# When the whole blocks of the second weights are stored: by rounding progress, or in four fixed steps

## The chip, the cores and the metric

The kernel runs on one core of a Trainium2 chip. The metric is the device time of one launch in microseconds, as the median of several runs; lower is better.

## The reference

Inputs are q, k, v of shape 8 x 8 x 576 x 64 (batch, heads, rows, width), and two weight matrices in float64, 512 x 2048 and 2048 x 512. Three things are computed, one after the other:

```
attention in chunks of 64 rows:  out = softmax(q k^T / 8) v        per head and chunk
x = out, heads side by side                                        8 x 576 x 512
u = x + Re(FFT over rows and columns of x)
y = u + relu(layernorm(u) @ w_ch1) @ w_ch2
```

All results are float32, while the weights arrive as float64.

## The kernel before, in words

**Tiles and groups.** The 8 x 576 rows are cut into tiles of 128 rows. Tiles are joined into nine groups of four, `g` = 0 to 8; groups 0 to 7 hold the main tiles of one batch each, the last holds the left-over rows of all batches. For each group the two matmuls of the MLP ("up" with the first weights, "down" with the second) run on PE, and between their parts the attention and the Fourier stage of the *next* batch are woven in by hand.

**Steps.** `mlp(g)` is a generator that yields after each part of a group's matmuls. The main loop counts these yields in `t` and, in the body of each step, lets the other work of that step be issued. For group 0 the steps 1 to 16 are parts of "up" (L1219) and the steps 17 to 32 are the 16 blocks `m` of "down" (L1260), so that block `m` comes just before the body of step 17 + `m`. `begin[1]` is 32, `ready_at[0]` is 27. Nothing is reordered afterwards: each engine and each DMA queue gets its instructions in the order in which the bodies issue them, and waits are set by the data and the spaces they touch.

**Rounding the weights.** The float64 weights are loaded in 32 pieces of 128 x 512 (512 KB each, L348, issued by SP): pieces 0 to 15 are the first weights, piece 16 + `m` is block `m` of the second weights. `round_weight(i)` turns a piece into float32 with instructions on DVE (L372, L379, L380, L382, L388) and ACT (L364, L367, L370); its first half treats piece `i`, its second half finishes piece `i - 1`, whose raw space then takes the next load. The last pieces have only three raw spaces, in the rows of `xall`. `n_w` is the number of the next call of `round_weight`. In most steps there are one or two such calls; in step 23 one of them stands inside the Fourier stage of batch 1, ahead of `z_joined` (L752).

**The products with fewer multiplications.** From group 1 on (for "up") and group 2 on (for "down") the kernel multiplies in 2 x 2 blocks with seven products instead of eight, and later with fewer still. It needs the blocks of the second weights in DRAM (`s2`): three of the seven are plain blocks of the weights, four are sums of them.
- `keep2_whole(i)` (L1109) stores the three plain blocks for the rows `m` = 2`i`, 2`i` + 1 and 8 + 2`i`, 9 + 2`i`, with three DMAs of 256 KB from SP (L1114). Called W0 to W3 below. The rows must have been rounded.
- `keep2(i)` makes the four sums on POOL (L1095) in spare rows: of `xall`, which are the raw spaces of the last weight pieces, or of `yall`. `keep2_store` (L1107) stores them from SP in a later step. `keep2(1)` begins in the first step whose `n_w` is over 32.
- `keep1(p)` (L1078, POOL) makes sums of the first weights, writing them into the place of the second weights' blocks 0 to 11 (`keep1(0)`: blocks 0 to 2); `keep1_store` (L1082, SP) stores one block of the first weights. Such a store in step 24, say, is called K24.

**Where the whole blocks are stored.** The stores of `keep2_whole(i)` are issued in the step in which `n_w` passes 26 + 2`i`, after that step's roundings and before its `keep2_store` and `keep1_store`. More than one `i` may fall into a step.

**The rest around it.** In steps 23 to 27 the Fourier stage of batch 1 ends: its halves are joined on DVE (L752, L756), copied by ACT (L747, L773 to L778), multiplied on PE (`mix`, L840), copied and joined by ACT (L845) and DVE (L850, L851), added to x by DVE or POOL (L857), and normalized (L705 to L710, L998). The normalized rows are transposed on PE (L399) for group 1.

Of the kernel before, what the change touches and what calls it, by code (L numbers as in the profile page):

```python
# [16 lines left out]
def kernel(  # L17
# [43 lines left out]
    KF = DFF // 128  # L61
# [41 lines left out]
    NO, HF = 7, KF // 2  # L103
# [918 lines left out]
    def combined(g, q_, late=False):  # L1022

        unT = unTs[g]
        cl, ch = slice(q_ * 128, (q_ + 1) * 128), slice(256 + q_ * 128, 256 + (q_ + 1) * 128)
        b11, b12, b21, b22 = unT[:, 0:2, cl], unT[:, 0:2, ch], unT[:, 2:4, cl], unT[:, 2:4, ch]
        t1, t2, t4 = (tt_1[o][:, :, cl] if g == 1 else tt[:, o, :, cl] for o in range(3))
        if late:
            nc.vector.tensor_tensor(out=t4, in0=b21, in1=t2, op=ALU.subtract)
            return  # L1030
        nc.vector.tensor_tensor(out=t1, in0=b12, in1=b11, op=ALU.subtract)
        nc.vector.tensor_tensor(out=t2, in0=b22, in1=t1, op=ALU.subtract)
        nc.vector.tensor_tensor(out=b12, in0=b22, in1=b12, op=ALU.subtract)
        if g > 1:
            nc.vector.tensor_tensor(out=t4, in0=b21, in1=t2, op=ALU.subtract)
# [35 lines left out]
    def keep1(pair):  # L1071

        a11, o2, o1, a21, a12, o4, a22 = parts1(pair)
        for out_, in0, in1, op in (
            (o1, a21, a22, ALU.add), (o2, o1, a11, ALU.subtract),
            (a21, a11, a21, ALU.subtract), (o4, a12, o2, ALU.subtract),
        ):
            nc.gpsimd.tensor_tensor(out=out_, in0=in0, in1=in1, op=op)  # L1078

    def keep1_store(pair, o):  # L1080
        to = s1[pair, o].rearrange("p (k x) -> p k x", k=2)
        nc.sync.dma_start(out=to, in_=parts1(pair)[o])  # L1082
# [19 lines left out]
    def keep2_store():  # L1102
        to = s2.rearrange("o p (m e) -> o p m e", m=HF)
        while kept:
            m, made = kept.pop(0)
            for o, a in made:
                nc.sync.dma_start(out=to[o, :, m:m + 2], in_=a)  # L1107

    def keep2_whole(i):  # L1109

        m = 2 * i
        to = s2.rearrange("o p (m e) -> o p m e", m=HF)
        for o, m0, e0 in ((0, m, 0), (4, HF + m, 0), (5, HF + m, HM)):
            nc.sync.dma_start(out=to[o, :, m:m + 2], in_=w2[:, m0:m0 + 2, e0:e0 + HM])  # L1114
# [60 lines left out]
    def fetch(which):  # L1175
        i = n_slab[which]
        if which == 1 and i < HF // 2 * NO * (NG - 2):
            pair, o = divmod(i % (HF // 2 * NO), NO)
            nc.sync.dma_start(out=slab1[i % NS1].rearrange("p k r f -> p (k r f)"), in_=s1[pair, UP[o]])
        elif which == 3 and i < NR2 * (NG - FEW):  # L1180
            to = slab3[i % NS3].rearrange("p m e -> p (m e)")
            nc.sync.dma_start(out=to, in_=block_of(PRODUCTS[i % NR2][1]))
        elif which == 2 and i < NO * (FEW - first_of[2]):
            nc.sync.dma_start(out=slab2[i % NS2].rearrange("p m e -> p (m e)"), in_=s2[i % NO])
        n_slab[which] = i + 1
# [267 lines left out]
    def mlp(g):  # L1453

        for h1 in up_halves(g) if g >= first_of[1] else up_plain(g) if g > 0 else up_first():
            yield
        yield from (down_few if g >= FEW else down_halves if g >= first_of[2] else down_plain)(g, h1)

    with tc.manual_schedule():
# [22 lines left out]
        n_w = 2  # L1482
# [10 lines left out]
        def round_next(later=None):  # L1493
            nonlocal n_w
            if n_w <= len(pieces):
                round_weight(n_w, later)
                n_w += 1
# [25 lines left out]
        ready_at = [begin[g] + (2 * KF - 5 if g < first_of[2] else 2 * HF + 4) for g in range(NG)]  # L1523
# [12 lines left out]
        n_whole, n_kept, late, rest_ = 0, 0, [], None  # L1536
        conv2 = chain(conv2)
        t = 0
        for g in range(NG):
            for _ in mlp(g):  # L1540
                t += 1
                heavy = False
                for do in late:
                    do()
                late = []
                if t == 8:
                    nc.scalar.copy(tk, early_tk[:, :, :, 0:NE])
                if cur < len(sides):
                    t0 = 3 if cur == 0 else ready_at[cur - 1]
                    t1 = ready_at[cur]  # L1550
                    due = min(sizes[cur], (t - t0) * sizes[cur] // (t1 - t0))
                    if cur == 0:
                        due = late_due.get(t, (t - t0) * sizes[cur] // (t1 - 2 - t0))
                    while done < due:
                        heavy = next(sides[cur], None) or heavy
                        done += 1
                    if t >= t1:
                        for _ in sides[cur]:
                            pass
                        cur, done = cur + 1, 0  # L1560
                while joined:
                    combined(*joined.pop(0))
                if not heavy:
                    round_next(late if t < KF and t % 4 == 3 else None)
                    if t <= 2 or t < KF and t % 4 == 0 or t >= KF + 3:
                        round_next()

                while n_whole < HF // 2 and n_w > KF + HF + 2 * n_whole + 2:
                    keep2_whole(n_whole)
                    n_whole += 1  # L1570
                keep2_store()
                if n_w > len(pieces):
                    for _ in range(3):
                        next(conv2, None)
                if t == begin[1] - 1:
                    for _ in conv2:
                        pass
                    keep2_store()
                if begin[1] < t < begin[1] + 7 and t % 2:
                    keep1((t - begin[1] + 1) // 2)  # L1580
                if t == ready_at[FEW - 1]:
                    rest_ = make_rest()
                if t >= ready_at[FEW - 1]:
                    next(rest_, None)
                if t == begin[FEW] + 2 * HF - 2:
                    for _ in rest_:
                        pass
                    slab3.extend(
                        one_p.tile([128, Z3], FP32, tag=tag, name="more").rearrange("p (m e) -> p m e", m=4)
                        for tag in ("q", "k")  # L1590
                    )
                for _ in range((2, 3, 10, 11, 12, 12, 13, 13, 14, 15).count(t - begin[FEW])):
                    fetch(3)
                for _ in range(2 if t > begin[1] else 0):
                    if put_off:
                        b, t0_, r, o = put_off.pop(0)
                        nc.sync.dma_start(out=out[b, t0_ + 1 - r:t0_ + CH:2, :], in_=o)
                if KF < t <= KF + 4 or KF + 8 <= t < KF + 16:
                    keep1_store(n_kept // 3, (0, 4, 6)[n_kept % 3])
                    n_kept += 1  # L1600
                if begin[1] <= t < begin[1] + KF:
                    keep1_store((t - begin[1]) // 4, (2, 1, 3, 5)[(t - begin[1]) % 4])
                if t in (begin[1] + 9, begin[1] + 13, begin[1] + 16):
                    fetch(2)
                if t == begin[1] + KF:
                    for _ in range(NS1):
                        fetch(1)
# [49 lines left out]
```

## Time and profile before

| | |
|---|---|
| median of 3 runs | 1063.99 us (1063.61 to 1064.34) |
| the profiled execution | 1063.73 us, span on the core 1061.9 us |
| PE busy | 1043.3 us, 98% of the span |
| DVE busy | 626.5 us, 59% |
| POOL busy | 431.9 us, 41% |
| ACT busy | 315.5 us, 30% |
| bytes moved by DMA | 219.10 MB, mean 206 GB/s |
| stores of whole blocks (L1114) | 12, issued from 140.4 to 160.9 us of the span |

The span is the time in which the core's engines work; the run's time holds 1.8 us more around it. Times of the views are counted from the span's start. A matmul in float32 stands in the profile as more than one instruction: one block of "down", four matmuls, has eight.

### The profile page before, as it was taken

What the parts mean: (1) busy time and instruction counts of PE and PEld (TensorE: products, weight loads), DVE (VectorE), ACT (ScalarE), POOL (GpSimd) and SP (SyncE); (2) the same over time, 40 slices, a digit from 0 to 9 for tenths busy, and PEclk for the clock granted to TensorE, in tenths of its full rate; (3) what the DMA queues carried; (4) which work ended last, traced back from release to release, by engine and by line L of the source; (5) the groups of instructions that cost most, each with busy time, mean ns of one, the idle gap of its engine ahead of it and who ended that gap; (6) DMA issues with size and microseconds to landing.
All of it is one profiled execution on the core that took longest, in us unless ns stands there. A gap on an engine that the chain in (4) does not pass through costs nothing.

```text
span 1061.9 us, 20222 instructions
## 1 busy us (share of the span) xinstructions
PE 1043.3 (98%) x7482; PEld 851.6 (80%) x7482; DVE 626.5 (59%) x1339; ACT 315.5 (30%) x744; POOL 431.9 (41%) x555
## 2 busy tenths in 40 slices
PE   7999999999999999999999999999999999999998
PEld 6645444788888888888888888888888888888887
DVE  4798986974567465664565645745664666443332
ACT  4688573233113311332022312331133103201200
POOL 3410119753425151244134421514252777660282
PEclk9999999999999999999999999999999999999999
DMA  8767675687688447973678357944753759998364
GB/s 169 221 197 213 163 218 199 203 233 230 231 215 230 134 142 214 250 207 108 186 229 223 118 169 231 250 131 155 215 168 102 269 187 353 363 399 279 89 216 142
DMA packets 167088, 219.10 MB, mean 206 GB/s; under 512 B 77228, under 2 KB 111020, under 8 KB 161614
## 3 DMA queue, kind: packets, MB, share of 16 engines
q1 hardware_dynamic: 155978, 211.98, 64.8%
q0 software_dynamic: 9024, 4.91, 2.1%
q8 instruction: 60, 0.98, 0.4%
q10 hardware_dynamic: 1988, 0.92, 0.3%
q14 instruction: 38, 0.31, 0.1%
HBM read 183.61 MB, written 34.08 MB: 205 GB/s over the span
## 4 chain that ended last, share of the span: by engine, by line
PE 79%; DVE 6%; DMA 4%; ACT 3%; POOL 3%; SPq 2%; issue 2%; DVEq 0%; ACTq 0%; POOLq 0%
PE pa L1309 20%; PE pb L1309 15%; PE pb L1363 14%; PE pa L1363 11%; PE dn L1427 7%; PE pt L399 2%; SPq L265 2%; PE mix L840 2%; PE xp L501 2%; PE z L722 1%; DMA xall<-in_moe_w_ch_dram 1%; PE up L1219 1%; PE sc L451 1%; POOL h L1207 1%; POOL part L1156 1%
## 5 line engine op out<-in xcount | busy, mean ns | idle before, releaser
L1309 PE MATMUL pa<-unT,wa 128*128 128x256 f32 x736 | 175.3, 381 | 0.2 <-DVE xall L1317 0.2
L1309 PEld LDWEIGHTS pa<-unT,wa 128*128 128x128 f32 x736 | 138.1, 190 | 19.6 <-DVE xall L1317 0.6
L1309 PE MATMUL pb<-wa 128*128 128x256 f32 x448 | 106.6, 381 | 0.0
L1309 PEld LDWEIGHTS pb<-wa 128*128 128x128 f32 x448 | 84.3, 190 | 11.5
L1363 PE MATMUL pa<-wb,h 128*128 128x256 f32 x384 | 87.2, 380 | 0.0
L1363 PE MATMUL pb<-wb,h 128*128 128x256 f32 x384 | 86.4, 379 | 0.0
L1193 POOL TENSOR_TENSOR h<-h 128x256 f32<-128x256 f32 x48 | 40.8, 858 | 98.2 <-DVE wb L1191 91.6
L1363 PEld LDWEIGHTS pa<-wb,h 128*128 128x128 f32 x384 | 71.8, 190 | 9.7
L1363 PEld LDWEIGHTS pb<-wb,h 128*128 128x128 f32 x384 | 72.0, 190 | 9.4
L1044 POOL DMA_DIRECT2D out_dram<-wb x28 | 18.8, 674 | 121.8 <-DVE wb L1380 71.9
L1315 DVE TENSOR_TENSOR wa<-pb,wa 128x256 f32<-128x256 f32 x56 | 23.7, 424 | 63.5 <-ACT wa L1314 63.5
L1309 PE MATMUL pb<-unT,wa 128*128 128x256 f32 x256 | 60.6, 379 | 0.1
L1325 ACT ACTIVATE h<-pa 128x256 f32<-128x256 f32 x64 | 24.6, 384 | 115.0 <-PE pa L1309 114.1
L1260 PE MATMUL dn<-wb,h 128*128 128x512 f32 x128 | 58.7, 608 | 0.0
L1314 ACT COPY wa<-pa 128x256 f32<-128x256 f32 x56 | 20.9, 372 | 121.4 <-PE pa L1309 121.4
L1309 PEld LDWEIGHTS pb<-unT,wa 128*128 128x128 f32 x256 | 48.6, 190 | 7.1 <-DVE wa L1315 0.5
L1207 POOL TENSOR_TENSOR h<-h 128x512 f32<-128x512 f32 x34 | 42.8, 1276 | 27.2 <-ACT h L1331 24.1
L1309 PE MATMUL pa<-wa 128*128 128x256 f32 x224 | 53.9, 383 | 0.0
L483 ACT COPY pT<-pt 128x512 f32<-128x512 f32 x36 | 21.0, 582 | 105.8 <-PE pt L399 105.5
L1331 ACT ACTIVATE h<-h 128x512 f32<-128x512 f32 x64 | 40.0, 630 | 39.5 <-DVE h L1330 39.1
L1219 PE MATMUL up<-unT,wa 128*128 128x512 f32 x108 | 49.4, 598 | 0.0
L857 POOL TENSOR_TENSOR xall<-y,xall 128x513 f32<-128x513 f32 x14 | 22.3, 1590 | 61.1 <-DVE y L851 45.0
(312 smaller groups left out, 2136.6 us busy)
## 6 DMA issues: line engine op xcount, KB each, us to landing
wa<-s SPq DMA_DIRECT2D x196, 256.0 KB
wb<-s SPq DMA_DIRECT2D x42, 1024.0 KB
wb<-s SPq DMA_DIRECT2D x32, 512.0 KB
xall<-in_moe_w_ch_dram SPq DMA_DIRECT2D x22, 512.0 KB
q<-in_q_dram SPq DMA_DIRECT2D x96, 112.0 KB
k<-in_k_dram SPq DMA_DIRECT2D x96, 112.0 KB
s<-part SPq DMA_DIRECT2D x32, 256.0 KB
v<-in_v_dram SPq DMA_DIRECT2D x124, 64.0 KB
```

The lines of the kernel that those rows point to most:

```text
L265: eng.dma_start(out=t[p0:p0 + np_], in_=src[b, :, c * CH:c * CH + np_, :].rearrange("h p d -> p h d"))
L857: eng.tensor_tensor(out=x[:, 0:w], in0=y[:, 0:w], in1=x[:, 0:w], op=ALU.add)
L1193: nc.gpsimd.tensor_tensor(out=h1[:, m, hi], in0=h1[:, m, lo], in1=h1[:, m, hi], op=ALU.subtract)
L1207: eng.tensor_tensor(out=out_, in0=a, in1=b, op=op)
L1219: nc.tensor.matmul(out=up, lhsT=w1[:, kk, m * 128:(m + 1) * 128], rhs=unT[:, kk], start=(kk == 0), stop=(kk == KD - 1), skip_group_check=True,
L1260: nc.tensor.matmul(out=dn, lhsT=h1[:, m, s * 128:(s + 1) * 128], rhs=w2[:, m, :], start=(m == 0), stop=(m == KF - 1),)
L1309: nc.tensor.matmul(out=dst, lhsT=w[:, kk, r], rhs=rhs[o][:, kk], start=(o in (0, 1) and kk == 0), stop=(kk == 1), skip_group_check=True,)
L1315: nc.vector.tensor_tensor(out=b, in0=pbs[r][:, 0], in1=a, op=ALU.add)
L1325: nc.scalar.activation(out=h1[:, m, lo], in_=dst, func=ACTF.Relu)
L1331: nc.scalar.activation(out=h1[:, HF + m], in_=h1[:, HF + m], func=ACTF.Relu)
L1363: nc.tensor.matmul(out=dst, lhsT=lhs[:, m], rhs=w[:, m], start=(o in (0, 2) and m == 0), stop=(m == HF - 1), skip_group_check=True,)
L1427: nc.tensor.matmul(out=dst, lhsT=lhs[:, m], rhs=w[:, m], start=(fresh and not half and m == 0), stop=(m == 3), skip_group_check=True,)
```

## The change

The condition under which `keep2_whole` is called no longer looks at how many pieces have been rounded. From step 24 on, one call is made in each step until all four have been made: W0 in step 24, W1 in 25, W2 in 26, W3 in 27. By then all 32 pieces have been loaded and rounded in program order. Within a step the place is the same as before, and each call issues the same three DMAs.

```
-                while n_whole < HF // 2 and n_w > KF + HF + 2 * n_whole + 2:
+                if n_whole < HF // 2 and t > ready_at[0] - 4:
                     keep2_whole(n_whole)
                     n_whole += 1
                 keep2_store()
```

## The prediction

> **What bounds the kernel now.** I read the page first: PE is busy 98% of the span, so only a few places can give or lose anything, and the slices with holes are the first ones. The view of windows then singles out the stretch in which the last pieces of the second weights are rounded (columns: length, then busy us and instruction count of PE, PEld, DVE, ACT, POOL; granted clock, DMA share, GB/s):
>
> ```profile
> 116.50:145.00 28.50, 28.50 (x184) 13.74 (x184) 25.36 (x64) 16.09 (x26) 0.44 (x4) 1.00 0.71 171
> 145.00:152.00 7.00, 7.00 (x39) 3.45 (x33) 4.46 (x10) 5.14 (x12) 0.00 (x0) 1.00 1.06 329
> 152.00:166.00 14.00, 11.53 (x34) 6.04 (x33) 10.69 (x18) 5.58 (x17) 9.14 (x7) 0.88 0.64 202
> 166.00:192.00 26.00, 23.93 (x168) 12.39 (x167) 19.05 (x28) 10.09 (x28) 21.52 (x17) 1.00 0.60 208
> ```
>
> PE idles 2.47 us in the third row and 2.07 us in the fourth, and its clock sags to 0.88 in the third. To see who makes it wait I followed the chain of waits back through these stretches (start, us, what):
>
> ```profile
> 136.86 4.52 DMA xall<-in_moe_w_ch_dram
> ...
> 143.06 6.75 DMA xall<-in_moe_w_ch_dram
> ...
> 152.40 0.68 DVE zs L752
> ...
> 159.85 1.48 POOL xall L1095
> ...
> 164.52 1.24 POOL xall L857
> ...
> 171.24 1.69 POOL xall L857
> ```
>
> So from 143 to 182 us the end is not set by PE but by one raw weight piece in flight for 6.75 us (piece 30), the DVE rounding that waits for it, the joining of the Fourier halves queued behind that rounding on DVE (L752), the last rounding, the combined blocks on POOL (L1095), and the sum into x queued behind them on POOL (L857). Why was this piece 2.2 us slower than the one before it? SP's own timeline answers (start, us, instruction):
>
> ```profile
> 136.86 3.53 SPq L348 DMA_DIRECT2D xall<-in_moe_w_ch_dram  x2
> 140.44 1.53 SPq L1114 DMA_DIRECT2D s<-wb  x3
> 142.02 0.63 SPq L1082 DMA_DIRECT2D s<-wa  x1
> 143.06 3.66 SPq L348 DMA_DIRECT2D xall<-in_moe_w_ch_dram  x2
> 146.77 14.62 SPq L1114 DMA_DIRECT2D s<-wb  x9
> 161.44 0.52 SPq L1082 DMA_DIRECT2D s<-wa  x1
> 162.06 2.10 SPq L1107 DMA_DIRECT2D s<-xall  x4
> ```
>
> The first whole block, W0 (three stores of 256 KB), goes out just ahead of pieces 30 and 31 (143.06); W1 to W3 follow, and then hold SP until 160.9 because they wait for the last roundings.
>
> **What the Trainium skill says.** "DMA: Bandwidth & Descriptors", section "Queues, rings and completion order": on each DMA engine the descriptors of a queue are consumed in ring order. So a load issued behind stores starts behind them. The trace agrees: 4.52 us with little ahead, 6.75 us with W0 and one more store ahead. "TensorE: Matmul & The Clock Gate", Part 1: a free-running window of 3413 ns with PE idle puts it at half clock. The trace has this: after the idle 2.47 us the clock of 156 to 158 us is 0.51. The same page's opening table says that ACT and DVE take their instructions strictly in order, is what lets a rounding hold up L752; here L752 starts within 0.1 us of the rounding's end at 152.40.
>
> **The change, part by part.** Nothing is added or removed: the same 12 stores leave from the same places. Steps count as in the code. K stores in SP's line above are those of steps 17 to 20 and, at 161.44, 24; so W0 now goes out in step 20, W1 after the next two roundings, W2 and W3 in 23. Afterwards W0 to W3 go out in steps 24, 25, 26, 27.
>
> (1) W0 leaves the front of pieces 30 and 31. Piece 30's issue stays at 143.06: it waits for DVE to free its space (142.95 to 143.03), and that rounding waited for piece 28, landed 141.38, before W0 had moved anything. Its flight becomes that of its neighbours: 4.0 us (issued 134.38, used 138.40), 4.52, 4.65 (140.05 to 144.70). I take 4.4, so it lands at 147.45 instead of 149.81: **2.35 us** earlier, bounds 2.1 to 2.75. As a check, W0's 768 KB at the 329 GB/s of that stretch are 2.3 us. DVE is free by 147.3 (it ends piece 28's rounding), so it takes the piece at once.
>
> (2) What hangs on it. DVE's rounding of 2.57 us ends at 150.0, L752 may start: its input from ACT (L747) is ready at 148.84, so ACT doesn't hold it. Piece 31, issued 146.4 behind 30 and now ahead of W0, lands by about 150.9 and is wanted at 151.5. All later links of the chain follow each other on DVE, ACT and POOL with the same durations, so each comes 2.35 earlier: mix ready 152.9, POOL's L1095 at 157.5, L857 at 162.2 and 168.9, and the last transpose of the normalized rows, which waits until 182.38 now, at 180.0.
>
> (3) PE. Its wait of 2.47 before mix shrinks to about 0.2 (the block before ends 152.77), and with it goes the half clock, which made the next block take 4.91 instead of 3.60. That looks like 2.3 + 1.3 + 0.4 = 4 us, but is not kept: PE then runs 152.95, mix 1.1, block 3.6, mix 1.1, block 3.5, mix 1.1, block 3.6 = 166.95, and must wait for the next transpose, whose PSUM space DVE frees at 171.08 now and 168.75 then. It waits 1.8 us where it waited 0.40. If that again costs half clock (up to 1.7 us), two further waits of 0.53 and 1.14 stand behind it and swallow nearly all: 0 to 0.5 lost, I take 0.
>
> (4) W0 to W3 where they go. W0, K24 and W1 leave between 146.8 and 150.5; their data is rounded by 144. W2 and W3 stand between the combined stores: SP has POOL's first set by 161, then W2 and W3 at 0.5 us an issue (1.5 each) fit before the second set is ready at 167. In the DMA engines they add 1.57 MB, 4.4 us at the 357 GB/s of 162 to 164 us, to a stretch already full; I cost it at nothing, because who waits has room: POOL needs the first set's space again at 176 (it is stored near 166), the second's at 181 (near 174). POOL's overwrite of blocks 0 to 2 (L1078, 172.88 now) waits for W0 and W1, landed by about 153. If these covers are gone, a late landing passes 1:1 into POOL and the stores behind it. SP's stall from 146.8 to 160.9 goes; it held only stores that POOL made later, worth 0.
>
> Sum: −2.35 us at the start of the next group, which PE enters without a gap (191.39 now). After it, everything is placed relative to PE or behind it in order, so it stays to the end. The profiled execution took 1063.73 us (span 1061.9); 1063.73 − 2.35 = 1061.4. The median of the runs shown is 0.26 higher, so I forecast **1061.6**.
>
> **Rivals.** *Load not freed (no measurable change).* Piece 30 is slow because of the K store or because reads of HBM are slow there, not W0. For it: piece 29, with W0 issued right behind, still took 4.65. Against: W0 is three quarters of the bytes ahead. With the K store alone to blame it lands near 149, gain 0.8; 1062.9. Here too belongs a flight of 4.65 or more, gain up to 2.1.
>
> *More than forecast.* Piece 29 and with it 30's issue come 0.3 earlier, because W0 no longer mixes with 29, and one of the late waits vanishes: 3 us, 1060.7.
>
> *Slower.* W2 and W3 before the second combined set delay its landing, so that POOL's L1095 at 183.39 (181 then) waits for its space; its four stores then hold SP, behind which stand the loads of the next batch (k, issued 190.74). It decides only if that set lands after 181, against 174 by my sum; to lose 2.1 net it must land at 185.5, which means 130 GB/s instead of 357. Price then: about 1066.
>
> *The change doesn't do what it says:* W0 might be in step 24 anyway; SP's order above excludes it.
>
> **How the numbers follow.** 0.2% of 1063.99 is 2.13 us, about what a measurement of this kernel tells from no change; my forecast lies only just past it, at 1061.86. Chances: the forecast chain 0.58 (of which 0.06 fall short of 2.13), more than forecast 0.06, load not freed 0.27, slower 0.09. Faster 0.58, same 0.33, slower 0.09. The likeliest case alone spans 1061.2 to 1061.9; the range goes to 1060.7 for the bigger gain and to 1063.6 for a load hardly freed, leaving out the slower case and the rest.
>
> **What would show it.** Right: the load issued near 143.06 takes about 4.4 us; no whole-block store ahead of it on SP; L752 near 150; the wait before mix below 0.5 and no 0.5 clock at 156; a new PE wait of some 1.8 us before the first transpose of normalized rows; the next group's first matmul near 189. Wrong: that load still takes over 6 us; or POOL's L1095 after 176 waits for a store; or the group starts at 189 but the span is not shorter.

## The result, and the profile after

The changed kernel takes 1061.28 us (median of 12 runs, 1059.76 to 1063.28) against 1064.32 us of the kernel before on the same chip (12 runs, 1062.93 to 1065.31): ratio 0.9977, 95% interval 0.9969 to 0.9985, or 2.4 us less. (The two medians as they stand lie 3.0 us apart, ratio 0.9971, which is inside the interval.) The forecast was 1061.6, faster by 2.35. In microseconds the interval is a gain of 1.6 to 3.3, so the time alone does not tell the forecast from two of its rivals, a load that is freed less than expected (gain up to 2.1) and a bigger gain (3); the trace has to. PE, DVE, ACT and POOL issue the same instructions in the same order; only the order on SP differs.

The profiled execution of the changed kernel has a span of 1058.9 us. The view of windows over the same stretches (columns as before):

```profile
116.50:145.00 28.50, 28.50 (x196) 13.94 (x194) 25.39 (x64) 15.89 (x26) 0.43 (x4) 1.00 0.64 170
145.00:152.00 7.00, 7.00 (x26) 3.00 (x20) 6.72 (x14) 5.86 (x14) 0.00 (x0) 1.00 0.79 232
152.00:166.00 14.00, 13.80 (x49) 7.63 (x48) 8.65 (x14) 6.25 (x22) 11.88 (x9) 1.00 0.71 226
166.00:192.00 26.00, 22.22 (x164) 12.41 (x164) 21.04 (x33) 8.60 (x23) 21.51 (x20) 1.00 0.71 233
```

Between 145 and 152 us DVE is busy for 6.72 us where it was 4.46, because it no longer waits for the raw piece, and the engines move 232 GB/s where they moved 329. PE's idle time of 152 to 166 us is down from 2.47 to 0.20 us, the sagging clock is gone with it, and that of 166 to 192 us has grown from 2.07 to 3.78 us.

The chain of waits (start, us, what), with the same links as before:

```profile
136.40 4.68 DMA xall<-in_moe_w_ch_dram
...
142.75 4.32 DMA xall<-in_moe_w_ch_dram
...
149.66 0.68 DVE zs L752
...
157.11 1.48 POOL xall L1095
```

Piece 30 flies 4.32 us instead of 6.75, and L752 starts 2.7 us earlier. This execution was already 0.46 us ahead at the first block of "down" (116.01 against 116.47), where nothing had changed yet. SP's timeline shows the moved stores:

```profile
139.93 0.52 SPq L1082 DMA_DIRECT2D s<-wa  x1
142.75 3.50 SPq L348 DMA_DIRECT2D xall<-in_moe_w_ch_dram  x2
146.31 1.55 SPq L1114 DMA_DIRECT2D s<-wb  x3
147.90 0.95 SPq L1082 DMA_DIRECT2D s<-wa  x1
148.90 2.10 SPq L1114 DMA_DIRECT2D s<-wb  x3
155.90 5.01 SPq L1107 DMA_DIRECT2D s<-xall  x4
160.97 0.52 SPq L1082 DMA_DIRECT2D s<-wa  x1
161.54 1.72 SPq L1114 DMA_DIRECT2D s<-wb  x3
```

W0 stands behind pieces 30 and 31, W1 behind K24, W2 behind the first combined set. What PE made of it is in its own timeline (start, us, instruction, in brackets the idle time before it and who ended it). First the kernel before:

```profile
155.25 0.49 PE L840 MATMUL mix<-ce,zf 128*128 128x129 f32 x2 [2.47 <-ACT zf L773]
156.83 4.91 PE L1260 MATMUL dn<-wb,h 128*128 128x512 f32 x8
...
171.21 0.63 PE L399 MATMUL pt<-ident,un 128*128 128x128 f32 x4 [0.40 <-DVE y L851]
175.81 0.63 PE L399 MATMUL pt<-ident,un 128*128 128x128 f32 x4 [0.53 <-DVE y L851]
...
182.38 0.66 PE L399 MATMUL pt<-ident,un 128*128 128x128 f32 x4 [1.14 <-ACT unT L1013]
```

Then the changed kernel:

```profile
152.52 0.49 PE L840 MATMUL mix<-ce,zf 128*128 128x129 f32 x2 [0.20 <-ACT zf L773]
...
153.73 3.60 PE L1260 MATMUL dn<-wb,h 128*128 128x512 f32 x8
...
168.50 0.63 PE L399 MATMUL pt<-ident,un 128*128 128x128 f32 x4 [2.10 <-DVE y L851]
...
173.09 0.63 PE L399 MATMUL pt<-ident,un 128*128 128x128 f32 x4 [0.53 <-DVE y L851]
...
179.66 0.66 PE L399 MATMUL pt<-ident,un 128*128 128x128 f32 x4 [1.14 <-ACT unT L1013]
```

The 2.27 us off the wait before mix, 0.37 off mix itself (1.58 us from its start to the next block's before, 1.21 after) and 1.31 off that block are 3.95 us on PE, but the wait before the first transpose takes 1.70 back: 2.25 stay. The next two waits are the same to the hundredth, as in a chain that is shifted as a whole.

### The profile page after: what moved, and what is told of

It is laid out like the page before. It is cut to its first block, busy times and chain, and to the rows that moved or that the text cites. A ratio compares the mean times of both kernels' runs of the same rounds, so it can differ in the third digit from the quotient of the medians.

```text
span 1058.9 us, 20224 instructions
## 1 busy us (share of the span) xinstructions
PE 1042.0 (98%) x7482; PEld 851.4 (80%) x7482; DVE 625.7 (59%) x1339; ACT 315.2 (30%) x744; POOL 432.9 (41%) x555
## 3 DMA queue, kind: packets, MB, share of 16 engines
q0 software_dynamic: 9024, 4.91, 2.1%
## 4 chain that ended last, share of the span: by engine, by line
PE 81%; DVE 5%; DMA 4%; SPq 3%; ACT 3%; POOL 2%; issue 1%; DVEq 0%; ACTq 0%; POOLq 0%
PE pa L1309 20%; PE pb L1309 15%; PE pb L1363 14%; PE pa L1363 11%; PE dn L1427 9%; PE pt L399 2%; DMA xall<-in_moe_w_ch_dram 2%; PE up L1219 2%; PE xp L501 2%; PE mix L840 2%; PE z L722 1%; SPq L265 1%; PE sc L451 1%; POOL part L1156 1%; DVE power L380 1%
## 5 line engine op out<-in xcount | busy, mean ns | idle before, releaser
L1309 PE MATMUL pa<-unT,wa 128*128 128x256 f32 x736 | 175.3, 381 | 0.2 <-DVE xall L1317 0.2
L1309 PEld LDWEIGHTS pa<-unT,wa 128*128 128x128 f32 x736 | 138.1, 190 | 19.6 <-DVE xall L1317 0.6
L1309 PE MATMUL pb<-wa 128*128 128x256 f32 x448 | 106.6, 381 | 0.0
L1309 PEld LDWEIGHTS pb<-wa 128*128 128x128 f32 x448 | 84.3, 190 | 11.5
L1309 PE MATMUL pb<-unT,wa 128*128 128x256 f32 x256 | 60.6, 379 | 0.1
L1260 PE MATMUL dn<-wb,h 128*128 128x512 f32 x128 | 57.4, 596 | 0.0
L1309 PEld LDWEIGHTS pb<-unT,wa 128*128 128x128 f32 x256 | 48.6, 190 | 7.1 <-DVE wa L1315 0.6
L1309 PE MATMUL pa<-wa 128*128 128x256 f32 x224 | 53.9, 383 | 0.0
L857 POOL TENSOR_TENSOR xall<-y,xall 128x513 f32<-128x513 f32 x14 | 22.3, 1591 | 61.1 <-DVE y L851 46.8
```

What stands on the lines that cost most here:

```text
L857: eng.tensor_tensor(out=x[:, 0:w], in0=y[:, 0:w], in1=x[:, 0:w], op=ALU.add)
L1260: nc.tensor.matmul(out=dn, lhsT=h1[:, m, s * 128:(s + 1) * 128], rhs=w2[:, m, :], start=(m == 0), stop=(m == KF - 1),)
L1309: nc.tensor.matmul(out=dst, lhsT=w[:, kk, r], rhs=rhs[o][:, kk], start=(o in (0, 1) and kk == 0), stop=(kk == 1), skip_group_check=True,)
```

## The experiments

Ratios are to the kernel before, beside which each ran. Since executions differ by some tenths of a microsecond before step 20, the traces are compared by two distances from the first matmul of "down" (L1260): to L752, and to the first up matmul of group 1 (L1309). They are worked out from the starts in the timelines; before: 152.32 − 116.47 = 35.85 and 191.39 − 116.47 = 74.93 (from the unrounded starts). "Between" is the way from L752 to group 1. Each kernel has one profile, the changed one two, and these two differ by 0.55 us in both distances; a smaller difference between two kernels is not read as an effect. Of the edits the lines that matter are shown; parameters that `keep2_whole` was given for them (which array, which of its stores, which engine) are left out.

| kernel | ratio (95% interval) | to L752 | to group 1 | between |
|---|---|---|---|---|
| before | 1 | 35.85 | 74.93 | 39.08 |
| changed | 0.9977 (0.9969 to 0.9985) | 33.57 | 72.68 | 39.10 |
| changed, again | 0.9980 (0.9973 to 0.9986) | 33.02 | 72.11 | 39.09 |
| only W0 moved | 0.9968 (0.9957 to 0.9979) | 33.61 | 72.69 | 39.08 |
| only W1 to W3 moved | 0.9996 (0.9988 to 1.0005) | 35.32 | 74.39 | 39.07 |
| W0 twice | 1.0022 (1.0014 to 1.0030) | 38.73 | 77.81 | 39.08 |
| PE kept busy | 1.0000 (0.9990 to 1.0010) | 35.78 | 74.84 | 39.06 |
| a third of W0 early | 0.9982 (0.9974 to 0.9990) | 33.61 | 72.69 | 39.08 |
| W2, W3 twice | 0.9980 (0.9974 to 0.9987) | 32.92 | 72.00 | 39.07 |
| W0 from ACT | 0.9997 (0.9985 to 1.0008) | 35.75 | 74.81 | 39.05 |
| K stores late | 0.9968 (0.9958 to 0.9977) | 32.47 | 71.56 | 39.10 |
| sums later | 0.9964 (0.9951 to 0.9978) | 33.32 | 70.91 | 37.59 |
| both of these | 0.9966 (0.9957 to 0.9975) | 32.11 | 69.67 | 37.57 |

**Which stores matter: one half of the change at a time.** The theory: W0 ahead of piece 30 is all of it. The rival: SP no longer stands for 14.6 us at W1 to W3. Only W0 moved:

```
                 while n_whole < HF // 2 and n_w > KF + HF + 2 * n_whole + 2:
-                    keep2_whole(n_whole)
-                    n_whole += 1
+                    n_whole += keep2_whole(n_whole) is None if n_whole > 0 else 1
+                if t == KF + 8:
+                    keep2_whole(0)
```

> Only W0 is moved (to step 24); W1 to W3 go out where they did before the change. If piece 30 was late because W0 stood ahead of it, this alone gives the whole gain: its flight falls from 6.75 to about 4.4 us, L752 starts near 150, ratio to before 0.9977 (-2.4 us). If the gain came from SP no longer standing at W1 to W3 (14.6 us), it is gone: ratio 1.000, because that stall stays.

Measured: 0.9968. Its chain of waits has the short flight, while SP still stands at L1114 for 13.8 us (146.0 to 159.8):

```profile
135.84 5.59 DMA xall<-in_moe_w_ch_dram
...
143.11 3.44 DMA xall<-in_moe_w_ch_dram
...
149.14 0.68 DVE zs L752
```

The flight of 3.44 us must not be read alone: piece 28 (the first line) was late here, although no W0 was about, and piece 30 was issued late behind it. It landed 31.10 us after the first block of "down", as in the changed kernel (31.06) and 2.2 us before its time in the kernel before (33.34).

The counterpart, only W1 to W3 moved (against the changed kernel):

```
-                if n_whole < HF // 2 and t > ready_at[0] - 4:
+                if n_whole == 0 and n_w > KF + HF + 2 or 0 < n_whole < HF // 2 and t >= KF + 8 + n_whole:
                     keep2_whole(n_whole)
                     n_whole += 1
```

> The counterpart: W0 stays in step 20, W1 to W3 are moved to steps 25, 26, 27. If W0 ahead of the load is the cause: piece 30 still flies about 6.7 us, the wait of about 2.5 us before mix stays, ratio 1.000 within 0.0010. If the freed SP is the cause: ratio 0.9977 and the wait before mix gone.

Measured: 0.9996, no change. Here SP's stall is gone and nothing is gained: the wait before mix is still 1.94 us and group 1 comes only 0.54 earlier, which is within the spread of two profiles. W0's place carries the effect; the rival falls. The flight itself, 5.17 us from an issue at 143.50, was shorter than the expected 6.7, because the issue came late: what counts is when the piece lands.

**The dose.** W0 twice in step 20, the second time to a spare array in DRAM:

```
-                    keep2_whole(n_whole)
+                    for into in (None, s2x) if n_whole == 0 else (None,):
+                        keep2_whole(n_whole, into)
```

> The kernel before with W0 stored twice in step 20, the second time to a spare place in DRAM: 768 KB more ahead of piece 30. If the bytes ahead in the queue set its flight, it grows by as much again as W0 cost, 2.3 us, to about 9 us, and the kernel takes 2 to 2.5 us longer than before, ratio 1.0022. If only the presence of a store ahead matters, or something else in that stretch, the flight stays near 6.7 and the ratio is 1.000.

Measured: 1.0022, as expected, and group 1 comes 2.9 us later than before. The flight, 7.38 us, is not the 9 that was expected, because SP's own issue was held up to 144.24; the piece lands 2.9 us later than before all the same:

```profile
144.24 7.38 DMA xall<-in_moe_w_ch_dram
...
154.21 0.68 DVE zs L752
```

The smaller dose, one of W0's three stores in step 20 and the other two in step 24:

```
-                if n_whole < HF // 2 and t > ready_at[0] - 4:
-                    keep2_whole(n_whole)
-                    n_whole += 1
+                if n_whole == 0 and n_w > KF + HF + 2 and t <= KF + 4 or n_whole < HF // 2 and t > ready_at[0] - 4:
+                    early = t <= KF + 4
+                    keep2_whole(n_whole, which=(0,) if early else (1, 2) if n_whole == 0 else (0, 1, 2))
+                    n_whole += not early
```

> The changed kernel, but one of W0's three stores (256 KB) goes out in step 20 again, the other two in step 24. If the bytes ahead of piece 30 set its flight, a third of W0's cost comes back, 0.7 to 0.8 us: flight near 5.1 us, ratio to before 0.9984. If W0 as a whole has to be ahead, or its position only: ratio 0.9977 as the changed kernel, or 1.000 as the kernel before.

Measured: 0.9982. The timing cannot tell 0.9977 from 0.9984, and the trace tells little more. L752 comes 33.61 after the first block of "down". The five profiles in which all of W0 goes late and the K stores stay have 32.92 to 33.61, 33.29 on average, and a third of what W0 costs would be 0.8 us on top of that. So this profile shows 256 KB costing less than its share, 0 to 0.7 us, where 768 KB cost 2.2 to 2.8 us and the next 768 KB another 2.9. One profile beside a spread of 0.7 us does not settle whether the price starts from zero. A first store that drains before the load's own packets start would make it cheap; the windows of the kernel before, 102 GB/s from 140 to 142 us and 292 in the next two, do not contradict this, but it is argued and not shown.

**Queue or engines.** The kernel before, with W0's stores in step 20 issued by ACT:

```
-                    keep2_whole(n_whole)
+                    keep2_whole(n_whole, nc.sync if n_whole else nc.scalar)
```

> The kernel before with W0's three stores in step 20 issued by ACT instead of SP: the same bytes at nearly the same time, in another queue. If piece 30 is late because its descriptors stand behind W0's in SP's queue, it now shares the DMA engines with what is left of W0 and flies 4.5 to 5.5 us; ratio to before 0.998 to 0.999 (ACT loses some 1.5 us of issue time beside the path). If it is only a matter of bytes in the engines, whatever the queue: flight about 6.7 us and ratio 1.000.

Measured: 0.9997, and L752 is as late as before (35.75). The expectation of a gain missed: piece 30 flew 5.49 us, as in the first of the two expected cases, but the time is that of the second. DVE's timeline shows where it went:

```profile
142.25 0.43 DVE L372 TENSOR_SCALAR power<-xall 128x512 uint32<-128x512 uint32 x1 [1.77 <-DMA xall<-in_moe_w_ch_dram]
145.11 0.43 DVE L372 TENSOR_SCALAR power<-xall 128x512 uint32<-128x512 uint32 x1 [0.29 <-DMA xall<-in_moe_w_ch_dram]
149.42 0.43 DVE L372 TENSOR_SCALAR power<-xall 128x512 uint32<-128x512 uint32 x1 [1.74 <-DMA xall<-in_moe_w_ch_dram]
```

These are the starts of pieces 28, 29 and 30. DVE waits 1.77, 0.29 and 1.74 us for them, 3.80 in all; in the kernel before it was 0.44, 0.75 and 2.54, 3.73 in all, and in the kernel with only W0 moved 1.55 in all. So it is not W0's place ahead of piece 30 in SP's queue that costs: in another queue the same bytes at the same time cost as much. How the loss falls on the single pieces is not settled by this profile. That W0, in its own queue, gets in the way of piece 28 would fit, but piece 28 was as late with W0 gone altogether (1.55, only W0 moved) and with W0 in SP's queue (1.47, only W1 to W3 moved). What helped was to let these bytes move at another time.

**Was PE's half clock part of the price?** Twenty small matmuls ahead of the first mix, which overwrites them:

```
+            for _ in range(20 if (b, i) == (1, 0) else 0):
+                nc.tensor.matmul(out=mix[:, 0:128], lhsT=ident, rhs=ident, start=True, stop=True, skip_group_check=True)
```

> The kernel before with 20 small matmuls of the identity on PE ahead of the first mix (overwritten by it), which fill most of the idle 2.5 us there. Nothing else is moved. If PE is off the path there, as the prediction says: the half clock at 156 us is gone, the next block of down takes 3.6 instead of 4.9 us, and the time is the same, ratio 1.000 within 0.0010, because PE then waits longer for the first transpose of normalized rows (about 2 us). If the half clock was part of the price: ratio 0.9985 (-1.3 to -1.7 us).

Measured: 1.0000. PE's timeline of this kernel (in this kernel lines from the mix on stand two further down):

```profile
151.47 4.63 PE L835 MATMUL mix<-ident 128*128 128x128 f32 x40
155.93 0.39 PE L842 MATMUL mix<-ce,zf 128*128 128x129 f32 x2
...
157.04 3.60 PE L1262 MATMUL dn<-wb,h 128*128 128x512 f32 x8
...
169.99 0.63 PE L399 MATMUL pt<-ident,un 128*128 128x128 f32 x4 [0.29 <-DVE y L853]
```

The block takes 3.60 us again, so the half clock is gone. The filler took 4.5 us instead of the 2.2 I had meant, so that mix even starts late; therefore the transpose shows 0.29 us of waiting and not 2. So two things changed at once, the full clock (1.8 us won) and a late mix (1.9 us lost), and they cancel; the time of this kernel alone does not show what the clock is worth. The profiles together do. Mix starts 2.93 us after L752 in the kernel before, where its block then takes 4.91 us, 2.94 after it in the changed kernel, where the block takes 3.60, and 2.94 after it with W0 twice, where the block takes 5.49; with the filler it starts 4.83 after. Group 1 comes 39.06 to 39.10 us after L752 in all four. PE's time around the first mix is not on the path, with or without its clock.

**Do W2 and W3 hide where they went?** The yardstick first, the changed kernel unaltered:

> The changed kernel once more, as the yardstick for the three variants of it that share this chip: ratio to before 0.9977 (-2.4 us).

Measured: 0.9980. Then W2 and W3 twice in steps 26 and 27:

```
-                    keep2_whole(n_whole)
+                    for into in (None, s2x) if n_whole >= 2 else (None,):
+                        keep2_whole(n_whole, into)
```

> The changed kernel with W2 and W3 stored twice in steps 26 and 27, the second time to a spare place in DRAM: 1.57 MB, by the prediction's price 4.4 us, more in the stretch into which they were moved. If they hide there, as the prediction has it: ratio to before 0.9977 as the changed kernel. By the trace of the changed kernel POOL's L1095 at 175.7 has some 2.7 us of room, and 2.5 us of POOL idle before L1044 stand behind it, so up to 2 us of delay on POOL may be seen without a loss. If their place is on the path (the slower rival): 1.7 to 4.4 us longer than the changed kernel, ratio 0.999 to 1.002.

Measured: 0.9980, and group 1 is no later (72.00). The second combined set leaves SP at 168.9 instead of 165.7, and nobody waits for it. The slower rival of the prediction is refuted even at twice its load.

**What is left, and the path itself.** K17 to K20 behind the last loads too:

```
-                if KF < t <= KF + 4 or KF + 8 <= t < KF + 16:
+                for _ in range((KF + 8 <= t < KF + 16) + (KF + 12 <= t < KF + 16)):
                     keep1_store(n_kept // 3, (0, 4, 6)[n_kept % 3])
```

> The changed kernel with the stores K17 to K20 (256 KB each) too moved behind the last loads: two such stores in each of steps 28 to 31. In the changed kernel DVE still waits 0.6, 0.4, 0.6 and 0.25 us for pieces 27 to 30. If stores ahead of the loads are what is left of these waits, the flights fall to about 4.0 us, L752 comes 0.5 to 1 us earlier, and the ratio to before is 0.997. If the flights of 4.3 to 4.7 us are those of a load alone: ratio 0.9977 as the changed kernel.

(The waits for pieces 27 to 30 in the changed kernel's first profile are 0.52, 0.64, 0.61 and 0.25.) Measured: 0.9968; L752 0.55 to 1.1 us earlier than in the two profiles of the changed kernel, piece 30 flying 3.52 us. The kernel with both edits below has L752 earlier still (32.11). So the K stores, of which the prediction had the last one as a rival cause, have a part in the delay, together a smaller one than W0. Next, the combined sums begun one step later, so that on POOL the first sum into x stands behind three of them instead of five:

```
-                if n_w > len(pieces):
+                if n_w > len(pieces) and t >= KF + 8:
```

> The changed kernel with the combined sums of the second weights (L1095, POOL) begun one step later, in step 24 instead of 23. On POOL the first sum into x (L857) then stands behind three of them instead of five. If the path after L752 runs through POOL as the prediction's chain says: L857 starts near 158.9 instead of 161.8, the waits of PE before the first transposes shrink from 2.1 us to about 0, group 1 starts about 2.8 us earlier, ratio to before 0.9953. If POOL's order there is covered by something else (ACT's copies of mix, the roundings): ratio 0.9977 as the changed kernel. If the later combined sums come late for what needs them: slower than the changed kernel.

Measured: 0.9964. POOL's L857 starts where expected:

```profile
158.46 1.72 POOL L857 TENSOR_TENSOR xall<-y,xall 128x513 f32<-128x513 f32 x1
...
165.65 1.71 POOL L857 TENSOR_TENSOR xall<-y,xall 128x513 f32<-128x513 f32 x1 [3.01 <-DVE y L851]
```

This is the only edit that shortens the way from L752 to group 1, by 1.5 us, so POOL's order is on the path as the chain said. It is not the expected 2.8. PE's waits before the transposes fall from 2.10, 0.53 and 1.14 us to none, 0.38 and 1.13, which is 2.3 us, and 0.86 of that go into a new wait, for a transposed k that DVE makes behind the sums of group 1 (L1031 to L1033):

```profile
186.15 0.70 PE L451 MATMUL sc<-kT,qT 64*64 64x64 f32 x32 [0.86 <-DVE kT L418]
```

Both together:

> Both variants of the changed kernel together: K17 to K20 behind the last loads, and the combined sums begun in step 24. If the two gains are in a row on one chain they add: another 0.5 to 1 us against the later sums alone, ratio to before 0.9945. If PE is the bound by then, they don't add: ratio 0.9953.

Measured: 0.9966. Group 1 comes at 69.67, so there the gains do add, but the time does not follow. By their ratios all three lie 1 us or a little more below the changed kernel, but the intervals overlap its own, and the kernel with only W0 moved, whose distances are those of the changed kernel, stands at 0.9968 too. Between these kernels the timing leaves the order open.

## Why the prediction was right, point by point

*What bounds.* Right, and it held more exactly than the prediction could claim: from L752 to group 1 it is 39.05 to 39.10 us in all eleven profiles that leave POOL's order alone, whether L752 comes at 32.5 or at 38.7, and whether PE is cold, warm or stuffed with filler.

*(1) The flight of piece 30.* Predicted 4.4 instead of 6.75 us, measured 4.32. That W0 is the reason is shown by moving W0 alone, by leaving W0 alone in its place and by doubling it. How W0 does it was wrong in part. The prediction drew from the Trainium skill ("DMA: Bandwidth & Descriptors", "Queues, rings and completion order"), by which each DMA engine takes a queue's descriptors in ring order, that a load behind stores starts behind them. No run here speaks against that order, but it is not what costs: with W0 in ACT's queue the waits add up to the same 3.8 us. Here W0's bytes counted whichever of the two queues they came from. The check, 768 KB at 329 GB/s, is 2.4 us rather than 2.3 and near what W0 cost; whether it holds as a rate for a smaller store is open. The flight by itself was the wrong measure: between kernels with the same landing it ranged from 3.44 to 4.32 us, because the issue moved too.

*(2) What hangs on it.* Predicted L752 2.35 us earlier; by the distance from the first block of "down" it is 2.28. L1095 was expected at 157.5 and L857 at 162.2 and 168.9; they started at 157.11, 161.76 and 168.49, right once the 0.46 us is taken off by which this execution was ahead.

*(3) PE.* Wait before mix about 0.2: measured 0.20. The block at full clock: 3.60. A new wait of 1.8 before the first transpose: 2.10. That the nearly 4 us gained on PE would not be kept was the step on which the number hung, and it held. The further half clock that might have followed the new wait did not come: the clock is 1.00 from 152 to 192 us. So its price of nothing was not put to the test. On the half clock before, the prediction counts a window of 3413 ns with PE idle as agreeing with a wait of 2.47 us; a wait shorter than the window is not what it quotes (see the last section).

*(4) The moved stores.* Costed at nothing, measured at nothing, once and with W2 and W3 doubled. SP's stall costed at nothing: shown by the kernel in which only W1 to W3 move.

*The sum.* The start of group 1 was to come 2.35 us earlier; it came 2.25 (74.93 − 72.68) in one profile and 2.8 in the other. The profiled span fell by 3.0: 0.46 of it before the change could act, 2.25 here, and 0.27 late in the kernel. The ratio gives 2.4. That 2.35 and 2.4 agree to 0.1 us is luck: two profiles of the changed kernel differ by 0.55 at group 1, the interval of the ratio is 1.7 us wide, and the way from group 1 to the end, which the prediction took as fixed, was 870.5 us before and 870.2 and 872.7 in the two profiles of the changed kernel. What is not luck is the chain: the wait that goes, the wait that comes in its place and the constant way behind L752.

## What to carry to other kernels

Ask of every store that is issued early what load is under way or follows at once: a store that nobody waits for costs whatever it delays a load that an engine waits for, and moving it behind the last such load cost nothing here, where later traffic had room. Don't add up the idle time that an engine loses: follow the chain past it to the next wait that another engine ends, because what is gained up to there is limited by that engine's shift. Another queue for the same bytes at the same time was no remedy here (0.9997). And judge a load by when it lands, not by its flight.

## What the runs showed of the hardware that was not expected

Whether a wait of PE brings the half clock is not settled by its length. Before mix, waits of 2.47 us (before), 2.37 (W0 from ACT), 1.94 (only W1 to W3 moved) and 5.36 (W0 twice) were all followed by it. Before the first transpose, waits of 2.10 (changed, and two more kernels), 2.00, 1.90 and 1.46 were not. The half clock lasted 3.41 us in the first three and 6.83 in the last, worked out from the granted clock in slices of 0.2 us: one and two of the windows of 3413 ns of the Trainium skill ("TensorE: Matmul & The Clock Gate", Part 1). That page has the half clock come after a whole idle window; here 1.94 us of waiting were enough, so on this point the measurement differs. The windows run free by the same page, so that a wait can fall into one or be cut in two, which would fit the other waits; but the two kinds stand at different places of the kernel, the phase was not varied, and why the later place is spared stays open.

Late in the kernel the same program waits differently from one execution to the next. In the second profile of the changed kernel PE's timeline has

```profile
925.82 3.69 PE L1427 MATMUL dn<-xall,h 128*128 128x256 f32 x16 [1.48 <-DMA xall<-s]
932.02 1.97 PE L1427 MATMUL dn<-more,yall 128*128 128x256 f32 x8 [0.51 <-DVE wb L1437]
```

where the first one has no such waits. With all its gaps over 0.25 us that is 2.0 us, and 2.7 in the kernel with both variants: as much as the whole change. The waits for the last products' blocks explain at least in part why the span of the second profile was 1061.1 although its group 1 came 0.3 us earlier than in the first, and why a microsecond won early is hard to see in one execution's time.
